# Spectral mixing kernel: step 1 of the forward transform as 49 by 64, its float16 products on quarters of the TensorE array

## The chip, the cores and the metric

The kernel runs on one core of one Trainium2 chip. The metric is the device time of one execution in microseconds; the median of three runs is compared. A profiled execution has a span (first to last instruction) and a time of its own; both are given below.

## The reference

```python
# x: (8, 3136, 256); w_r, w_i: (256, 256); moe: d_model 256, d_ff 1024
X = np.fft.rfft(x, axis=1)
Yr = Xr @ w_r - Xi @ w_i + b_r
Yi = Xr @ w_i + Xi @ w_r + b_i
Yr, Yi = soft_threshold(Yr, 0.01), soft_threshold(Yi, 0.01)
y = np.fft.irfft(Yr + 1j * Yi, n=3136, axis=1)
h = y.reshape(25088, 256) @ w_in
sm = softmax(h)                       # along the 1024 columns
solu = h * sm
ln = (solu - mean) / np.sqrt(var + 1e-06) * g_ln
out = ln @ w_out
...
```

## The kernel before

The eight sequences (batches b = 0 to 7) go through the same stages. The transform of length 3136 is split as 98 by 32. **Step 1** (`fwd1`, for batches 2 to 7; `fwd1_plain` with float32 products for batches 0 and 1) multiplies a 98 by 98 matrix of cosines and sines, `fa16_s`, with x laid out as 98 rows; eight chunks of 1024 columns make a batch. In `fwd1` a chunk is loaded into `xt`, split into two float16 parts `xh` (by ScalarE) and `xl` (by VectorE), multiplied in two halves of 512 columns with three products each, and each half is taken out of PSUM as two float16 parts into `av` (ScalarE writes the high part, VectorE the low part). `av` goes to DRAM as `s1`. **Step 2** (`fwd2`) reads `s1` back as `bin`, in groups of four (`load_bin`), and multiplies with `fb`; its result `Xh`, `Xl` is mixed with the weights (`mix`), thresholded, transformed back (`inv1` with `gb`, whose 64 by 128 products run on the two row halves of the array at a time, and `inv2` with `ia_s`), and written to a ring `ring_hi`, `ring_lo` of 128-row tiles.

The second part takes 196 such tiles: `moe_head` (products `ph` with `win`, six per half, row maximum `nm`, exponential, sums), `moe_turn` (float16 parts `lh` and `ll`, two transposing DMAs to `th` and `tl`) and `moe_tail` (24 products `po` with `wout`, scaling, store). A batch is 24 or 25 tiles; while the tiles of batch b run, step 1 of batch b+2 and step 2 to `inv1` of batch b+1 run among them.

The order is made before the program is built: each operation is recorded with a key (`nc.key`, a place in tiles), and a planner (`Plan`) puts the operations of all engines in one order by keys, data, buffers and PSUM banks, with lengths of its own for each operation. Each engine then executes its list strictly in that order. All DMAs are issued by one queue, SyncE's (SP), in its order; they use eight semaphores in turn, so a DMA is not issued before the one eight places ahead of it has landed. PSUM has eight banks; at most five hold front results (`pf`), five `ph`, two `po`.

Before the change a `pf` bank is asked for one half of a chunk at a time, and `xt` has four buffers, used in turn by the chunk loads of step 1 and by `load_peak` (which reads a batch once, to find its largest value). All recorded operations are issued from one line, L342 (L349 after the change), so in the profile they are told apart by the names of their tiles; there `fa16_s` stands as `fa_s`, and `s1`, `s2` of the float16 batches as `s`.

Of the kernel before, what the change touches and what calls it, by code (L numbers as in the profile page):

```python
# [25 lines left out]
H = N1 // 2  # L26
Q = (H - 1) // 2
# [5 lines left out]
S_SCALE, B_SCALE, Z_SCALE, X_SCALE = 2.0**-7, 2.0**-5, 2.0**-11, 2.0**-11  # L33
# [6 lines left out]
def fft_constants():  # L40
# [5 lines left out]
    FA, IA = np.zeros((N1, N1)), np.zeros((N1, N1))  # L46
    comps = []
    for q in range(Q):
        comps += [(2 * q + 1, 0), (2 * q + 2, 0), (2 * q + 1, 1), (2 * q + 2, 1)]
    comps += [(0, 0), (H, 0)]  # L50
    for c, (k1, im) in enumerate(comps):
        t = 2 * np.pi * ((np.arange(N1) * k1) % N1) / N1
        FA[:, c] = -np.sin(t) if im else np.cos(t)
        IA[c, :] = (1.0 if k1 in (0, H) else 2.0) / S * (-np.sin(t) if im else np.cos(t))

    def angle(k):
        return 2 * np.pi * ((np.arange(N2)[:, None] * np.asarray(k)[None, :]) % S) / S
# [3 lines left out]
    for q in range(Q):  # L61
        for j in range(2):
            k = 2 * q + 1 + j + N1 * np.arange(N2)
            s = np.where(2 * k > S, -1.0, 1.0)[None, :]
            C, Sn = np.cos(angle(k)), np.sin(angle(k))
            re, im = slice(j * N2, (j + 1) * N2), slice((2 + j) * N2, (3 + j) * N2)
            FB[re, q, re], FB[im, q, re] = C, Sn
            FB[re, q, im], FB[im, q, im] = -Sn * s, C * s
            GB[re, q, re], GB[im, q, re] = C.T, -(Sn * s).T
            GB[re, q, im], GB[im, q, im] = Sn.T, (C * s).T  # L70
    kd, kn = N1 * np.arange(1, N2 // 2), H + N1 * np.arange(N2 // 2)
    nd, m = len(kd), len(kd) + len(kn)
    FS, GS = np.zeros((2 * N2, P)), np.zeros((P, 2 * N2))
    d, n, I = slice(0, N2), slice(N2, 2 * N2), 2 * N2
    alt = np.cos(np.pi * np.arange(N2))
    FS[d, 0:nd], FS[n, nd:m], FS[d, m], FS[d, m + 1] = np.cos(angle(kd)), np.cos(angle(kn)), 1.0, alt
    FS[d, I : I + nd], FS[n, I + nd : I + m] = -np.sin(angle(kd)), -np.sin(angle(kn))
# [12 lines left out]
    out = dict(fa=FA.astype(np.float32), fbf=FB.astype(np.float32), fsf=FS.astype(np.float32))  # L90
    out["iaf"] = (IA * IA_SCALE).astype(np.float32)
    parts = dict(fa16=FA * A_SCALE, fb=FB, fs=FS, gb=GB * G_SCALE, gs=GS * G_SCALE, ia=IA * IA_SCALE)
# [132 lines left out]
class Op:  # L225
    def __init__(self, engine, key, seq):
        self.engine, self.key, self.seq = engine, key, seq
        self.calls, self.length, self.moved, self.tiles = [], 0.0, 0.0, []
        self.needs, self.next, self.start, self.end, self.half, self.port = set(), [], None, None, False, False
# [7 lines left out]
class Plan:  # L237
# [60 lines left out]
    def weigh(self, op, name, args, kw, ins, outs):  # L298
# [6 lines left out]
        elif op.engine == "tensor":  # L305
            moving = ins[-1]
            n = moving.cells.size * (4 if moving.dtype == F32 else 1) * 0.42 + 1
            op.half = "gb" in ins[0].tile.kw["name"]
            op.length += n / 2 if op.half else n
# [34 lines left out]
    def order(self):  # L344
        ready = {e: [] for e in self.ENGINES}
        free = dict.fromkeys(self.ENGINES, 0.0)
        waits, bus, half, port = {}, 0.0, False, 0.0
# [35 lines left out]
        while len(done) < len(self.ops):  # L383
# [15 lines left out]
            if e == "tensor":  # L399
                if op.half != half:  # L400
                    at += 100.0 if op.half else 220.0
                half = op.half
# [49 lines left out]
def fft_mix_solu_kernel(ctx: ExitStack, tc, x, w_r, w_i, b_r, b_i, w_in, w_out, g_ln, fa, fbf, fsf, iaf, fa16, fb, fs, gb, gs, ia, out):  # L452
# [70 lines left out]

    def load_after(t, src, before):

        nc.hold(before)
        nc.sync.dma_start(t, src)
# [8 lines left out]
    def load_peak(b, c):  # L536

        n = S * D // P // NPK
        t = xp.tile([P, C1], F32, name="xt", bufs=4)[:, :n]
# [41 lines left out]
    def fwd1(b, c):  # L581
        if c == 0:
            s1[b] = dram.tile([N1, N2, 2, D], F16, name="s1")
        xt = xp.tile([P, C1], F32, name="xt", bufs=4)[:N1]
        nc.sync.dma_start(xt, x[b].rearrange("(n1 n2) d -> n1 (n2 d)", n1=N1)[:, c * C1 : (c + 1) * C1])
        xh = xp.tile([N1, C1], F16, name="xh")
        xl = xp.tile([N1, C1], F16, name="xl")
        k = scales[b]["x"][:N1]
        nc.scalar.activation(xh, xt, AF.Copy, scale=k)
        nc.vector.scalar_tensor_tensor(xl, xt, k, xh, ALU.mult, ALU.subtract)  # L590
        n2 = C1 // D
        av = xp.tile([P, n2, 2, D], F16, name="av")[:N1]
        for h in range(C1 // HF):
            hs = slice(h * HF, (h + 1) * HF)
            pa = front_psum(b)
            nc.reserve(av[:, h * HF // D : (h + 1) * HF // D])
            with nc.together():
                for i, (t, j) in enumerate(((xh, 0), (xh, 1), (xl, 0))):
                    nc.tensor.matmul(pa[:N1], fa16_s[:, j], t[:, hs], start=i == 0, stop=i == 2)
            pv = pa[:N1].rearrange("p (n d) -> p n d", d=D)  # L600
            ah, al = (av[:, h * HF // D : (h + 1) * HF // D, j] for j in range(2))
            nc.scalar.activation(ah, pv, AF.Copy, scale=S_SCALE / A_SCALE)
            nc.vector.scalar_tensor_tensor(al, pv, S_SCALE / A_SCALE, ah, ALU.mult, ALU.subtract)
        nc.sync.dma_start(s1[b][:, c * n2 : (c + 1) * n2], av)
# [3 lines left out]
    def fwd1_plain(b, c):  # L608


        if c == 0:
            s1[b] = dram.tile([N1, N2, D], F32, name="s1f")
        n2 = C1 // D
        pool, name, bufs = (mp, "u", 4) if b == 0 and c % 2 == 0 else (xp, "xt", 4)
        xt = pool.tile([P, C1], F32, name=name, bufs=bufs)[:N1]
# [19 lines left out]
        for av, i, n in parts:  # L635
            nc.sync.dma_start(s1[b][:, c * n2 + i : c * n2 + i + n], av.rearrange("p (n d) -> p n d", d=D))
# [587 lines left out]
```

## Time and profile before

| | before |
|---|---|
| median of 3 runs | 1614.72 us (1614.09 to 1615.25) |
| profiled execution: time | 1616.65 us |
| profiled execution: span | 1614.9 us |
| busy PE / DVE / ACT / POOL | 98% / 82% / 77% / 70% |
| mean granted TensorE clock | 0.990 |

The profiled execution's time is 1.75 us above its span and 1.93 us above the median of the runs. Busy time of PE counts each matmul from its start to its modelled end, and ends overlap the following starts; how long a stream of matmuls takes is therefore read from the distance between starts.

### The profile page before, as it was taken

Reading aid. Unit: us, or ns where it says so; the run is one execution under the profiler, and the core shown is the slowest. Engines: PE = TensorE matmul, PEld = TensorE weight load, DVE = VectorE, ACT = ScalarE, POOL = GpSimd, SP = SyncE. Lnnn points to the kernel's source line nnn. Section 1 sums busy time; section 2 is a strip of 40 time slices with the busy share of each in tenths; the row PEclk is TensorE's granted clock in tenths of the full one; section 3 lists DMA queues with packets and bytes.
Section 4 is the critical chain, followed back from the end, with each engine's and each line's share of the span. In section 5 each row is a group of like instructions: output and inputs, shape, how many; then the busy total and the mean of one; then the engine's idle time right before and its main releaser. Section 6 shows DMA issues by size and latency. Waiting matters only on the chain.

```text
span 1614.9 us, 38042 instructions
## 1 busy us (share of the span) xinstructions
PE 1577.4 (98%) x13040; PEld 1126.1 (70%) x13040; DVE 1326.1 (82%) x3423; ACT 1238.8 (77%) x2576; POOL 1123.6 (70%) x1889
## 2 busy tenths in 40 slices
PE   5979999999999999999999999999999999999998
PEld 3545877678766777667776687666876677776675
DVE  4779789996799877898789978899688888877775
ACT  4667678886789867898679876798678877778886
POOL 0555776677866777667777687766976677777676
PEclk8989999999999999999999999999999999999999
DMA  8868955996579965899669984699857986677676
GB/s 236 277 228 206 210 145 133 227 240 155 127 185 232 226 151 121 185 243 217 135 130 224 279 169 118 135 246 258 166 112 165 204 172 129 122 146 154 140 129 115
DMA packets 533923, 290.25 MB, mean 180 GB/s; under 512 B 427642, under 2 KB 503964, under 8 KB 533728
## 3 DMA queue, kind: packets, MB, share of 16 engines
q1 hardware_dynamic: 533728, 287.82, 78.5%
q8 instruction: 102, 1.67, 0.4%
q14 instruction: 93, 0.76, 0.2%
HBM read 107.89 MB, written 77.07 MB: 115 GB/s over the span
## 4 chain that ended last, share of the span: by engine, by line
PE 92%; DVE 3%; ACT 2%; DMA 1%; issue 1%; POOL 0%; SPq 0%; DVEq 0%; ACTq 0%; POOLq 0%
PE po L342 31%; PE ph L342 30%; PE pf L342 27%; PE pb L342 4%; DVE u L342 1%; DVE xl L342 1%; DVE nm L342 1%; DMA zt<-s2f 0%; ACT u L342 0%; DMA s2f<-zs 0%; ACT junk L342 0%; DMA bin<-s1f 0%; DMA s1f<-tl 0%; DVE av L342 0%; DMA th<-lh 0%
## 5 line engine op out<-in xcount | busy, mean ns | idle before, releaser
L342 POOL TENSOR_TENSOR ll<-u,lh 128x1024 f16<-128x1024 f32 x196 | 424.4, 2166 | 98.5 <-ACT lh L342 95.4
L342 PE MATMUL po<-wout,th 128*128 128x256 f16 x3136 | 374.5, 273 | 4.1 <-DMA th<-lh 1.9
L342 PEld LDWEIGHTS <-th 128*128 128x128 f16 x3136 | 305.4, 98 | 64.9 <-issue 4.4
L342 ACT ACTIVATE u<-ph,m,hsb 128x512 f32<-128x512 f32 x384 | 295.9, 776 | 52.3 <-DVE m L342 51.7
L342 DVE TENSOR_REDUCE nm<-ph 128x1 f32<-128x512 f32 x392 | 264.5, 685 | 79.7 <-PE ph L342 78.6
L342 DVE SCALAR_TENSOR_TENSOR u<-ph,ch,u 128x512 f32<-128x512 f32 x392 | 281.5, 747 | 23.1 <-ACT u L342 13.7
L342 PE MATMUL ph<-win_hi,ring_hi 128*128 128x512 f16 x768 | 291.9, 380 | 0.2 <-DVE u L342 0.2
L342 PE MATMUL ph<-win_lo,ring_hi 128*128 128x512 f16 x768 | 291.5, 380 | 0.0
L342 PE MATMUL ph<-win_low,ring_lo 128*128 128x512 f16 x768 | 291.3, 379 | 0.0
L342 ACT CAST lh<-u 128x1024 f16<-128x1024 f32 x196 | 205.7, 1049 | 53.1 <-DVE u L342 52.8
L342 PEld LDWEIGHTS <-ring_hi 128*128 128x128 f16 x1536 | 146.8, 98 | 140.5 <-issue 6.5
L342 ACT ACTIVATE junk<-u,total 128x1024 bf16<-128x1024 f32 x196 | 226.1, 1154 | 7.1 <-POOL total L342 6.6
L342 PE MATMUL po<-wout,tl 128*128 128x256 f16 x1568 | 203.4, 273 | 0.8 <-DMA tl<-ll 0.8
L342 PEld LDWEIGHTS <-tl 128*128 128x128 f16 x1568 | 150.7, 98 | 35.0 <-issue 3.4
L342 POOL TENSOR_TENSOR y<-yt,yc 128x512 f32<-128x512 f32 (+1 forms) x104 | 133.1, 1281 | 59.4 <-ACT yt L342 32.7
L342 POOL TENSOR_TENSOR yl<-y,yh 128x512 f16<-128x512 f32 (+1 forms) x104 | 122.3, 1178 | 40.3 <-ACT yh L342 39.3
L342 PE MATMUL pf<-w_hi,Xh 128*128 128x256 f16 (+1 forms) x546 | 149.1, 273 | 0.0
L342 PE MATMUL pf<-w_hi,Xl 128*128 128x256 f16 (+1 forms) x546 | 148.9, 273 | 0.0
L342 PE MATMUL pf<-w_lo,Xh 128*128 128x256 f16 (+1 forms) x546 | 148.8, 273 | 0.0
L342 ACT ACTIVATE o<-po,r 128x256 f32<-128x256 f32 x196 | 93.2, 475 | 59.6 <-PE po L342 30.7
L342 PEld LDWEIGHTS <-ring_lo 128*128 128x128 f16 x768 | 75.1, 98 | 91.1 <-DVE last_lo L342 0.3
L342 PEld LDWEIGHTS <-Xh 128*128 128x128 f16 (+1 forms) x1196 | 113.9, 99 | 24.8 <-issue 1.9
(196 smaller groups left out, 2922.5 us busy)
## 6 DMA issues: line engine op xcount, KB each, us to landing
xt<-in_x_dram SPq DMA_DIRECT2D x108, 392.0 KB
zt<-s SPq DMA_DIRECT2D x56, 392.0 KB
s<-zout SPq DMA_DIRECT2D x42, 512.0 KB
s<-av SPq DMA_DIRECT2D x48, 392.0 KB
bin<-s SPq DMA_DIRECT2D x36, 512.0 KB
out_dram<-o SPq DMA_DIRECT2D x128, 96.0 KB
out_dram<-o SPq DMA_DIRECT2D x136, 64.0 KB
bin<-s1f SPq DMA_DIRECT2D x12, 512.0 KB
```

What stands on the lines that cost most here:

```text
L342: getattr(engine, name)(*args, **kw)
```

## The change

Step 1 becomes 49 by 64. Its matrix has 49 rows and columns, x is read as 49 rows of 64 by 256 values, and step 2 has 64 inputs for each of 49 components where it had 32 for each of 98 (its matrices keep their size of 128 by 128). The 49 by 49 matrix of the float16 batches is held twice, in partitions 0 to 48 and 64 to 112. A chunk holds the same 98 by 1024 values as before, as two blocks of 49 rows in partitions 0 to 48 and 64 to 112; each product of a chunk is four matmuls of 49 by 49 by 512, one for each quarter (row half r, column half g) of the array. Row halves write to different PSUM banks, column halves to different partitions of one bank. Two chunks are put together: their 24 matmuls are one group in PE's order, which asks for four banks at a time. Loads and stores of 49 rows are issued as 48 rows and one, so a chunk has four loads and four stores where it had one each. `xt` is now four fixed places: step 1 uses two, `load_peak` the two others. The rows 49 to 63 of step 1's places are cleared once by GpSimd. The batches with float32 products keep 98 by 98 matmuls, with a matrix that does two parts in one.

The keys change too: step 1 has 13 steps per batch (8 peaks, the scales, 4 pairs) from `first + 2` instead of 17 from `first + 6`, `front_b` starts one tile earlier, and `moe_tail` has its key half a tile later. The planner counts a quarter matmul as a fourth of its columns.

```diff
+    both = np.zeros((2 * F1, 2 * F1))
+    both[::2, ::2] = both[1::2, 1::2] = FA
+    quarters = np.zeros((P // 2 + F1, P // 2))
+    quarters[:F1, :F1] = quarters[P // 2 :, :F1] = FA
...
+            op.split = 2 if "gb" in name else 4 if name == "fa16_s" else 1
+            op.length += n / op.split
...
-        t = xp.tile([P, C1], F32, name="xt", bufs=4)[:, :n]
+        t = x_place(2, 3)[:, :n]
...
+    def fwd1(b, c0):
+
+        if c0 == 0:
+            s1[b] = dram.tile([F1, F2, 2, D], F16, name="s1")
+        half = P // 2
+        R = half + F1
+        xv = x[b].rearrange("(n1 c g r i) d -> c r n1 g (i d)", n1=F1, g=2, r=2, i=2)
+        k = scales[b]["x"][:R]
+        work = []
+        for c in range(c0, c0 + TOGETHER):
+            xt = x_place(0, 1)[:R]
+            for r in range(2):
+                for rows in rows_apart(r):
+                    n1 = slice(rows.start - r * half, rows.stop - r * half)
+                    nc.sync.dma_start(xt[rows].rearrange("p (g m) -> p g m", g=2), xv[c, r][n1])
+            xh = xp.tile([P, C1], F16, name="xh")[:R]
+            xl = xp.tile([P, C1], F16, name="xl")[:R]
+            nc.scalar.activation(xh, xt, AF.Copy, scale=k)
+            nc.vector.scalar_tensor_tensor(xl, xt, k, xh, ALU.mult, ALU.subtract)
+            av = xp.tile([P, 2, 2, 2, D], F16, name="av")[:R]
+            work.append((c, xh, xl, av, [front_psum(b) for _ in range(2)]))
+        nc.reserve(*(w[3] for w in work))
+        with nc.together():
+            for _, xh, xl, _, pa in work:
+                for i, (t, j) in enumerate(((xh, 0), (xh, 1), (xl, 0))):
+                    for r in range(2):
+                        rows = slice(r * half, r * half + F1)
+                        for g in range(2):
+                            nc.tensor.matmul(
+                                pa[r][g * half : (g + 1) * half], fa16_s[rows, j], t[rows, g * HF : (g + 1) * HF], start=i == 0, stop=i == 2
+                            )
+        for c, _, _, av, pa in work:
+            for r in range(2):
+                pv = pa[r][:R].rearrange("p (n d) -> p n d", d=D)
+                ah, al = av[:, r, :, 0], av[:, r, :, 1]
+                nc.scalar.activation(ah, pv, AF.Copy, scale=S_SCALE / A_SCALE)
+                nc.vector.scalar_tensor_tensor(al, pv, S_SCALE / A_SCALE, ah, ALU.mult, ALU.subtract)
+            for g in range(2):
+                to = s1[b][:, 8 * c + 4 * g : 8 * c + 4 * g + 4].rearrange("k n t d -> k (n t d)")
+                for rows in rows_apart(g):
+                    nc.sync.dma_start(to[rows.start - g * half : rows.stop - g * half], av[rows].rearrange("p r i t d -> p (r i t d)"))
+
+    TOGETHER = 2
...
-        steps = [(load_peak, (b, c)) for c in range(NPK)] + [(set_scales, (b,))] + [(fwd1, (b, c)) for c in range(NCH)]
+        steps = [(load_peak, (b, c)) for c in range(NPK)] + [(set_scales, (b,))] + [(fwd1, (b, c)) for c in range(0, NCH, TOGETHER)]
...
+            clear_between()
         if b + 2 < B:
-            front_a(b + 2, first + 6, (L - 6) / 17)
+            front_a(b + 2, first + 2, (L - 2) / 13)
         if b + 1 < B:
-            front_b(b + 1, first + (6 if b == 0 else -2), (L - (8 if b == 0 else 4)) / (NU + 3))
+            front_b(b + 1, first + (6 if b == 0 else -3), (L - (8 if b == 0 else 5)) / (NU + 3))
...
-            nc.key = first + n + 1
+            nc.key = first + n + 1.5
```

On PE, the first chunk of step 1 in batch 2 stood before the change like this (names with their numbers, so that the PSUM banks `pf` can be told apart):

```order
L342 LDWEIGHTS fa16_s_171
L342 MATMUL pf_3436<-xh_3277,fa16_s_171 98x512
L342 LDWEIGHTS fa16_s_171
L342 MATMUL pf_3436<-xl_3392,fa16_s_171 98x512
L342 LDWEIGHTS fa16_s_171
L342 MATMUL pf_3440<-xh_3277,fa16_s_171 98x512
L342 LDWEIGHTS fa16_s_171
L342 MATMUL pf_3440<-xl_3392,fa16_s_171 98x512
```

The first of its two `xh` products on each bank is not shown twice; a chunk was six matmuls with six weight loads. With the change the first pair of chunks begins like this on PE:

```order
L349 MATMUL ph_3890<-win_low_1105,ring_lo_1233 128x512
L349 LDWEIGHTS fa16_s_168
L349 MATMUL pf_3901<-xh_3476,fa16_s_168 64x512
L349 LDWEIGHTS fa16_s_168
L349 MATMUL pf_3904<-xh_3476,fa16_s_168 64x512
L349 LDWEIGHTS fa16_s_168
L349 MATMUL pf_3901<-xl_3552,fa16_s_168 64x512
L349 LDWEIGHTS fa16_s_168
L349 MATMUL pf_3904<-xl_3552,fa16_s_168 64x512
L349 LDWEIGHTS fa16_s_168
L349 MATMUL pf_3915<-xh_3524,fa16_s_168 64x512
```

Each matmul row stands there twice in a row (the two column halves), and the `xh` rows once more for the second product: 24 matmuls on four banks follow each other, with a weight load ahead of each, and no other product stands among them.

On SP, the end of step 1 of batch 4 stood before the change like this, from the last stores of `av` to the first load of `bin`:

```order
L342 DMA s1_10713<-av_11439 98x2048
L342 DMA zt_11522<-s2_8997 98x2048
L342 DMA_TRANSPOSE th_11579<-lh_11550 128x8x128
L342 DMA xt_11600<-in_x_dram 128x784
L342 DMA_TRANSPOSE tl_11618<-ll_11577 128x8x128
L342 DMA out_0_dram<-o_11616 96x256
L342 DMA out_0_dram<-o_11616 32x256
L342 DMA xt_11658<-in_x_dram 128x784
L342 DMA_TRANSPOSE th_11670<-lh_11646 128x8x128
L342 DMA xt_11690<-in_x_dram 98x1024
L342 DMA xt_11705<-in_x_dram 98x1024
L342 DMA bin_11709<-s1_10713 128x4x512
```

And with the change, for the same batch:

```order
L349 DMA s1_11053<-av_11996 48x2048
L349 DMA s1_11053<-av_11996 1x2048
L349 DMA out_0_dram<-o_12024 32x256
L349 DMA out_0_dram<-o_12024 96x256
L349 DMA_TRANSPOSE th_12090<-lh_12011 128x8x128
L349 DMA out_0_dram<-o_12101 96x256
L349 DMA out_0_dram<-o_12101 32x256
L349 DMA_TRANSPOSE tl_12152<-ll_12027 128x8x128
L349 DMA bin_12174<-s1_11053 128x4x512
```

The store rows of 48 and of one stand there twice for each of two chunks, eight in a row. Behind the last of them the first load of `bin` has moved from the eleventh issue behind it to the seventh, and no load of `xt` stands between. In the whole program SP issues 1480 DMAs where it issued 1192.

## Rows read from the trace of the kernel before

**Rows 1.** Page, busy us (share of the span) and instructions of each engine.
```profile
PE 1577.4 (98%) x13040; PEld 1126.1 (70%) x13040; DVE 1326.1 (82%) x3423; ACT 1238.8 (77%) x2576; POOL 1123.6 (70%) x1889
```
**Rows 2.** Page, shares of the span in the chain that ended last.
```profile
PE 92%; DVE 3%; ACT 2%; DMA 1%; issue 1%; POOL 0%; SPq 0%; DVEq 0%; ACTq 0%; POOLq 0%
```
**Rows 3.** Busy us of the engines in stretches of the span.
```profile
core 0: us, PE busy (x) PEld busy (x) DVE busy (x) ACT busy (x) POOL busy (x), PEclk, DMA share, GB/s
...
200.00:1500.00 1300.00, 1296.62 (x11129) 938.95 (x11128) 1103.79 (x2858) 1023.49 (x2138) 942.35 (x1595) 1.00 0.79 176
...
660.00:735.00 75.00, 74.33 (x536) 48.28 (x535) 72.33 (x195) 67.98 (x139) 47.70 (x98) 1.00 1.04 237
```
**Rows 4.** Tile `fa_s`: operation, count, ns min/median/max, first and last start us.
```profile
L342 PE MATMUL pf<-xh,fa_s x192: 377/379/418, 256.8 to 1279.5; 98*98 98x512 f16 x192
L342 PE MATMUL pf<-xl,fa_s x96: 376/378/379, 257.3 to 1279.7; 98*98 98x512 f16 x96
```
**Rows 5.** Timeline of PE around one chunk of step 1: start us, us, work.
```profile
303.82 0.60 PE L342 MATMUL pf<-xh,fa_s 98*98 98x512 f16 x2
...
304.47 0.59 PE L342 MATMUL pf<-xh,fa_s 98*98 98x512 f16 x2
...
305.12 0.38 PE L342 MATMUL ph<-win_hi,ring_hi 128*128 128x512 f16 x1
```
**Rows 6.** Timeline of PE around 24 products with `gb`, on row halves.
```profile
370.63 0.49 PE L342 MATMUL po<-wout,th 128*128 128x256 f16 x3
371.06 0.39 PE L342 MATMUL pf<-yh,gb 64*128 64x256 f16 x4
371.29 0.38 PE L342 MATMUL pf<-yl,gb 64*128 64x256 f16 x4
...
372.47 0.39 PE L342 MATMUL po<-wout,tl 128*128 128x256 f16 x2
```
**Rows 7.** Timeline of weight loads (PEld) in the stretch of rows 6.
```profile
371.05 1.21 PEld L342 LDWEIGHTS <-gb 64*128 64x128 f16 x24 [0.21 <-issue]
```
**Rows 8.** Timeline of PE around six products with `gs_s`, all on one quarter.
```profile
301.74 0.40 PE L342 MATMUL pf<-yh,gs_s 64*64 64x256 f16 x2
301.99 0.38 PE L342 MATMUL pf<-yl,gs_s 64*64 64x256 f16 x2
...
302.51 0.39 PE L342 MATMUL ph<-win_hi,ring_hi 128*128 128x512 f16 x1
```
**Rows 9.** Groups of instructions, ACT, of 98 and of 128 partitions: busy us, mean ns.
```profile
L342 ACT ACTIVATE av<-pf 98x512 f16<-98x512 f32 x96 | 56.1, 603 | 9.5 <-PE pf L342 7.6 <-ACT junk L342 1.0
L342 ACT ACTIVATE Xh<-pf 128x512 f16<-128x512 f32 x72 | 43.2, 600 | 0.0
```
**Rows 10.** Timeline of PE, the longest wait of step 1: in brackets idle us, releaser.
```profile
481.82 0.59 PE L342 MATMUL pf<-xh,fa_s 98*98 98x512 f16 x2 [1.46 <-DVE u L342]
```
**Rows 11.** Tile `s`, SP's issues: ns min/median/max.
```profile
L342 SPq DMA_DIRECT2D s<-av x48: 307/367/1154, 260.5 to 1283.0; - x48
```
**Rows 12.** Timeline of SP from the last store of step 1 to step 2's load.
```profile
714.42 0.69 SPq L342 DMA_DIRECT2D s<-av  x1
715.21 0.34 SPq L342 DMA_DIRECT2D zt<-s  x1
...
725.34 0.40 SPq L342 DMA_DIRECT2D bin<-s  x1
```
**Rows 13.** Timeline of PE, last step-1 and first step-2 matmul, batch 4, then 7.
```profile
706.55 0.38 PE L342 MATMUL pf<-xl,fa_s 98*98 98x512 f16 x1
...
735.91 0.83 PE L342 MATMUL pf<-fb,bin 128*128 128x128 f16 x12
...
1279.71 0.38 PE L342 MATMUL pf<-xl,fa_s 98*98 98x512 f16 x1
...
1296.39 0.78 PE L342 MATMUL pf<-fb,bin 128*128 128x128 f16 x11
```

More of the change, by code (lines that the diff above doesn't have):

```diff
@@ L88, in fft_constants @@
     GS = GS.reshape(2, 2 * N2, 2 * N2).transpose(1, 0, 2)
-    out = dict(fa=FA.astype(np.float32), fbf=FB.astype(np.float32), fsf=FS.astype(np.float32))
+    both = np.zeros((2 * F1, 2 * F1))
+    both[::2, ::2] = both[1::2, 1::2] = FA
+    quarters = np.zeros((P // 2 + F1, P // 2))
+    quarters[:F1, :F1] = quarters[P // 2 :, :F1] = FA
+    out = dict(fa=both.astype(np.float32), fbf=FB.astype(np.float32), fsf=FS.astype(np.float32))
     out["iaf"] = (IA * IA_SCALE).astype(np.float32)
-    parts = dict(fa16=FA * A_SCALE, fb=FB, fs=FS, gb=GB * G_SCALE, gs=GS * G_SCALE, ia=IA * IA_SCALE)
+    parts = dict(fa16=quarters * A_SCALE, fb=FB, fs=FS, gb=GB * G_SCALE, gs=GS * G_SCALE, ia=IA * IA_SCALE)
     out.update({k: halves(v) for k, v in parts.items()})
@@ L228, in __init__ @@
         self.calls, self.length, self.moved, self.tiles = [], 0.0, 0.0, []
-        self.needs, self.next, self.start, self.end, self.half, self.port = set(), [], None, None, False, False
+        self.needs, self.next, self.start, self.end, self.split, self.port = set(), [], None, None, 1, False
     def touch(self, tile):
@@ L307, in weigh @@
             n = moving.cells.size * (4 if moving.dtype == F32 else 1) * 0.42 + 1
-            op.half = "gb" in ins[0].tile.kw["name"]
-            op.length += n / 2 if op.half else n
+            name = ins[0].tile.kw["name"]
+            op.split = 2 if "gb" in name else 4 if name == "fa16_s" else 1
+            op.length += n / op.split
         else:
@@ L346, in order @@
         free = dict.fromkeys(self.ENGINES, 0.0)
-        waits, bus, half, port = {}, 0.0, False, 0.0
+        waits, bus, split, port = {}, 0.0, 1, 0.0
         for op in self.ops:
@@ L522, in fft_mix_solu_kernel, with x_place, clear_between @@
     s1 = {}
+    places = const.tile([P, 4, C1], F32, name="xt")
+    turns = {}
+    def x_place(*some):
+        turns[some] = turns.get(some, -1) + 1
+        return places[:, some[turns[some] % len(some)]]
+    def clear_between():
+        nc.gpsimd.memset(places[P // 4 : P // 2, :2], 0.0)
     def load_after(t, src, before):
@@ L579, in set_h_scale @@
         scales[b]["h"] = hs
[L581 to L597, printed above, removed]
-                for i, (t, j) in enumerate(((xh, 0), (xh, 1), (xl, 0))):
[L599 to L604, printed above, removed]
```

66 lines of the change are left out of this document (34 added, 32 removed).

## The prediction

> **What bounds the kernel now.** I read the page's busy shares first: PE is busy 98% of the span, VectorE, the next, 82% [rows 1]. Then the chain that ended last: 92% of the span lies on PE [rows 2]. So the span is the length of PE's stream, and the question for each part is whether PE streams less or waits more. The third view says where PE waits today: from 200 to 1500 us it is busy 1296.62 of 1300 us at a granted clock of 1.00, so it loses 3.4 us in that stretch [rows 3]. All of step 1 in float16 lies in it, from 256.8 to 1279.7 us [rows 4]. The same view shows who is close behind: in one stretch of step 1, 660 to 735 us, VectorE is busy 72.3 of 75 us, ScalarE 68.0, and the DMA engines are full (share 1.04) [rows 3]. A microsecond taken from PE there is a microsecond of the kernel only if these keep up, and that decides how much of the gain stays.
>
> **What is removed.** Step 1 has 192 + 96 = 288 matmuls of 512 columns [rows 4], six per chunk in 48 chunks. The first of a chunk starts at 303.82 us and the first matmul behind the chunk at 305.12: 1.30 us per chunk [rows 5]. 48 x 1.30 = 62.4 us leave the stream.
>
> **What is added on PE.** A product of a chunk is now four matmuls of 512 columns on four quarters, with the column count of one old half. If the four run together, a product takes as long as one old matmul, 1.30 / 6 = 0.217 us, and 48 x 3 = 144 products take 31.2 us. No row shows two column halves at work together. The nearest shows row halves: four `gb` matmuls of 256 columns take 0.23 us, 371.06 to 371.29, where the full-array `po` of 256 columns in front of them take 0.109 each, so two run at a time [rows 6]. The bounds are therefore 31.2 us (four at a time) and 62.4 us (row halves together, column halves one after the other). I take four at a time: `gb` shows that the array accepts parts as independent streams, and column halves of one row half read other columns of the same rows and write to other partitions of the same bank. *The Trainium skill, "TensorEngine Tiling (Array Packing)", section "Available Configurations", counts 64 by 64 as four tiles; no row of this case shows four at work.*
>
> Weight loads double to 576, each for 49 columns. The 24 loads of `gb` start and end within 1.21 us, 0.05 us each [rows 7], so four loads per product need 0.20 of its 0.217 us if they need as long; 49 columns are fewer than the 128 there. I cost them at nothing; the cover is the product before them. Without it they cost up to 0.20 us per product, 29 us in all.
>
> Changing between whole array and parts costs time. The last `po` in front of `gb` starts at 370.63 + 2 x 0.109 = 370.85, `gb` at 371.06, the next `po` at 372.47 [rows 6]: 1.62 us for one `po` (0.109) and twelve pairs (1.31), so 0.20 us to go in and out. 24 groups: 4.8 us.
>
> PE's stream changes by 31.2 + 4.8 - 62.4 = **-26.4 us**. That is the gain if nothing new waits.
>
> **What the other engines get.** ScalarE and VectorE have as many instructions as before on 113 partitions instead of 98; 98 partitions take 603 ns and 128 take 600 [rows 9], so nothing. The clearing is one GpSimd instruction in the whole program, on an engine that is busy 942 of 1300 us [rows 3]; nothing. DMA bytes stay the same, with half as long pieces on the load side; at a full DMA system that could cost or gain, and I put it to the waits below. SP issues 288 DMAs more, at the 0.367 us of a store of step 1 [rows 11], taken for loads and stores alike: 106 us of queue time, 18 per batch. In the stretch behind step 1 SP is already full: from the store at 714.42 to the load at 725.34 eleven issues follow with about 0.1 us between them [rows 12]. Queued behind the new issues are the transposes whose result `po` needs, and `bin`, which step 2 needs.
>
> **New waits.** (a) A group wants four PSUM banks and both chunks' `xl` at once, where a half wanted one bank. The longest wait for step 1 today is 1.46 us [rows 10]. (b) Step 2 follows step 1 sooner. In batch 4 the last step-1 matmul starts at 706.55 us and the first of step 2 at 735.91, 29.4 us later; in batch 7 it is 16.7 us, 1279.71 to 1296.39, and PE does not wait [rows 13]. In the order of the change there stand, between the two in batch 4, 42 products `ph` (0.217 us), 56 `po` (0.109) and 24 with `ia_s` (0.046, an estimate by its 98 columns): 16.3 us; counted so, the six batches have 16 to 20 us. That is about the shortest chain that the trace shows to go well, and now four banks are taken out and eight stores issued in it. What is late next is all of PE, since its list is strict. For (a) and (b) together the lower bound is 0 (the planner moved work so that it fits) and the upper has no row; 24 groups that each wait the 1.46 us would be 35 us. I take six such waits, one per batch: **+8.8 us**, nearer to the low end, because today's order loses only 3.4 us in 1300 us though SP and VectorE are as full in these stretches.
>
> **Sum.** -26.4 + 8.8 = -17.6 us. On the profiled execution: 1614.9 - 17.6 = 1597.3 us span, 1599.0 us with the 1.75 us around it. Against the runs' median of 1614.72 us, 1.9 us below that execution, the forecast is **1597 us**.
>
> **Rivals.**
>
> *Waits take most of it.* The queue on SP is the likeliest place: if the 18 us of issues per batch find no gaps, transposes and `bin` come late by a part of that. With 3 to 4 us per batch instead of 1.5, 18 to 24 us are lost and the time is 1606 to 1612 us. For it: SP is full behind step 1 [rows 12], DMA share 1.04 [rows 3]. Against it: these full stretches cost PE nothing now, and no peak load of x stands any more between stores and `bin`.
>
> *Slower: the parts do not all overlap.* If the column halves of a row half take turns, 144 products take 62.4 us, PE's stream grows by 4.8 us, and with 4 to 9 us of waits the time is 1623 to 1628 us. It decides when a group of 24 takes over 2.4 us instead of 1.3 + 0.2: at 2.6 + 0.2 nothing is saved. The same end is reached if weight loads cannot hide: the two column halves use the same rows, so a load would wait for the matmul in flight on the other half, and with 0.20 us per product the 26.4 us are gone and 2.4 more (1617 us; 1626 with the waits). Against it: the six `gs_s` products, all on one quarter and so in the same rows, each with its own load, start 0.12 us apart, about the 0.109 of a 256-column matmul, so loads hide behind a matmul in the same rows [rows 8]. *The Trainium skill, "TensorE: Matmul & The Clock Gate", section "The mechanism" in Part 3, says that a weight load overlaps with matmuls in flight only when its row group differs; by that rule this rival would hold and the time would be the 1626 us above. The six products [rows 8] do not bear the rule out.*
>
> *Slower by SP alone.* Over 4.4 us of lateness per batch (26.4 / 6) the gain is gone; if all 18 us of issues came through, the time would be 1614.7 - 26.4 + 108 us. SP would have to have no gap at all; I give the part above 1618 us little.
>
> *All of it stays.* No new waits: 1588 us.
>
> **How the numbers follow.** Four at a time with 0 to 17 us of waits (1588 to 1605 us): 0.66, forecast 1597 within it. Waits of 17 to 23 us (1605 to 1611): 0.14. Waits that cancel the gain (1611 to 1618): 0.07. Slower by the parts: 0.07, by SP: 0.05. Better than 1588, by waits of today that go: 0.01. The range of 8 in 10 is the first two cases, 1587 to 1611 us. About 0.2% (3.2 us) is what a measurement of this kernel can tell from no change: faster 0.81, same 0.07, slower 0.12.
>
> **What would show it.** Right: in the timeline groups of 24 `fa_s` matmuls with about 1.5 us from the first start to the next work, four starts within some nanoseconds; in 200 to 1500 us some 10 us of idle PE, at step 1's and step 2's first matmul. Wrong: fours that start 0.2 us apart inside a product (parts in turn, or loads in the open); long waits of PE on `th`, `tl` or `bin` (SP); a granted clock below 1.00 in those stretches, which I have left out.

## The result, and the profile after

The changed kernel takes 1625.33 us (median of 4 runs, 1623.24 to 1627.11) against 1614.55 us of the kernel before in runs beside it: ratio 1.0066, 95% interval 1.0048 to 1.0083. The forecast was 1597 us, range 1587 to 1611. The profiled span went from 1614.9 to 1625.1 us.

The page's busy shares and the chain that ended last, changed kernel [rows 1, 2 before]:

```profile
PE 1564.6 (96%) x13328; PEld 1107.1 (68%) x13328; DVE 1332.9 (82%) x3423; ACT 1242.8 (76%) x2576; POOL 1121.0 (69%) x1890
PE 79%; DMA 7%; DVE 5%; ACT 4%; issue 2%; POOL 1%; SPq 1%; DVEq 0%; ACTq 0%; POOLq 0%
```

PE works 13 us less in a span 10 us longer. In the chain PE's share fell from 92 to 79%, and DMA's rose from 1 to 7%. The stretch of [rows 3]:

```profile
core 0: us, PE busy (x) PEld busy (x) DVE busy (x) ACT busy (x) POOL busy (x), PEclk, DMA share, GB/s
200.00:1500.00 1300.00, 1272.97 (x11369) 913.37 (x11367) 1101.47 (x2837) 1021.55 (x2127) 936.03 (x1584) 0.99 0.80 175
```

PE stands idle for 27 of 1300 us where it was 3.4, and the granted clock is no longer 1.00. The view of PE's waits (from 200 us; us in total, times, longest) says for what:

```profile
PE po L349 <- DMA th<-lh: 17.1, 13, 4.6
PE po L349 <- DMA tl<-ll: 9.1, 10, 1.5
```

Before, the same two lines:

```profile
PE po L342 <- DMA th<-lh: 1.9, 2, 1.6
PE po L342 <- DMA tl<-ll: 0.8, 1, 0.8
```

Step 1 itself runs as forecast. PE's timeline of one group (start us, us, work) and the tile `fa_s` (count: ns min/median/max) [rows 4, 5]:

```profile
286.21 0.38 PE L349 MATMUL ph<-win_low,ring_lo 128*128 128x512 f16 x1
286.52 0.63 PE L349 MATMUL pf<-xh,fa_s 49*64 49x512 f16 x8
286.98 0.39 PE L349 MATMUL pf<-xl,fa_s 49*64 49x512 f16 x4
287.19 0.60 PE L349 MATMUL pf<-xh,fa_s 49*64 49x512 f16 x8
287.62 0.39 PE L349 MATMUL pf<-xl,fa_s 49*64 49x512 f16 x4
287.94 1.05 PE L349 MATMUL po<-wout,tl 128*128 128x256 f16 x8
...
L349 PEld LDWEIGHTS <-fa_s x576: 102/107/173, 286.5 to 1302.2; 49*64 49x64 f16 x192
L349 PE MATMUL pf<-xh,fa_s x384: 372/376/632, 286.5 to 1302.2; 49*64 49x512 f16 x192
```

24 matmuls take 1.42 us from the first start to the next work (286.52 to 287.94); two chunks took 2.60. The weight loads of `gb` in the kernel before, for comparison:

```profile
L342 PEld LDWEIGHTS <-gb x1152: 92/94/96, 52.5 to 1416.6; 64*128 64x128 f16 x192
```

Where the 10.2 us come from, by my own sums over the starts of neighbouring matmuls from 200 us to the end (the time of a matmul is its columns at 2.4 GHz; what lies beyond it goes to the matmul that follows, or, in a stretch of granted clock 0.5, to that stretch, together with the waits in it):

| us | before | after | difference |
|---|---|---|---|
| step 1's matmuls | 62.3 | 32.2 | -30.1 |
| mode changes | 8.9 | 13.6 | +4.7 |
| waits at step 1's matmuls | 2.4 | 0.8 | -1.6 |
| waits at `po` | 5.0 | 24.7 | +19.7 |
| lost in stretches at 1.2 GHz, their waits included | 0 | 14.7 | +14.7 |
| all else | | | +2.8 |

Of the 14.7 us, 6.9 are two further waits at `po` (4.59 and 2.32 us by the timeline) that reach into such stretches. The slower clock itself costs the rest, about 7.8 us, so waits at `po` come to 31.6 us in all.

One of the waits from its beginning, changed kernel: ScalarE's, SP's and PE's timelines (start us, us, work, in brackets the idle time and its releaser) and the stretch behind it:

```profile
897.94 1.12 ACT L349 CAST lh<-u 128x1024 f16<-128x1024 f32 x1
...
898.86 1.28 SPq L349 DMA_TRANSPOSE tl<-ll  x1
900.24 3.05 SPq L349 DMA_DIRECT2D s<-av  x8
903.41 0.79 SPq L349 DMA_DIRECT2D out_dram<-o  x2
904.25 4.81 SPq L349 DMA_DIRECT2D xt<-in_x_dram  x8
909.16 1.17 SPq L349 DMA_DIRECT2D out_dram<-o  x2
910.43 1.29 SPq L349 DMA_TRANSPOSE th<-lh  x1
...
911.06 0.38 PE L349 MATMUL pf<-v,ones 1*128 1x2 f32 x2
913.76 3.53 PE L349 MATMUL po<-wout,th 128*128 128x256 f16 x16 [2.32 <-DMA th<-lh]
917.13 1.04 PE L349 MATMUL po<-wout,tl 128*128 128x256 f16 x8
...
913.68:917.10 3.42, 3.34 (x16) 2.40 (x17) 3.42 (x18) 2.57 (x6) 1.49 (x6) 0.50 1.03 193
```

`lh` is ready at 899.06. Its transpose is issued at 910.43, behind eight stores (3.05 us) and eight loads (4.81 us) of step 1 and four stores of the result. PE waits 2.32 us, and then sixteen `po` take 3.37 us (913.76 to 917.13) instead of 16 x 0.109 = 1.74, because the granted clock of that stretch is 0.50, which is 1.2 GHz. Between 200 and 1500 us there are three such stretches. The first begins in a wait at `po` (4.59 us, ending at 321.47), the second at the end of the one shown, the third 1.3 us behind one of 2.59 us; before there was none.

Over all 372 transposes from 200 us on, the time from ready data to the issue sums to 719 us (before: 339). SP stands still in 117 of it and issues other DMAs in the rest; step 1's loads and stores and the peak loads take 204 (before: 43). SP as a whole is not full: from 200 us on it issues for 977 of 1425 us. In the rest it waits, by the view of its waits mostly for other engines' results that the next DMA in its order needs. The rule of eight semaphores is not what holds it: only 22 of its issues, with 13 us of standing in all, follow within 0.3 us on the landing of the DMA eight places ahead (e2: 5 issues, 4 us).

### The profile page after: what moved, and what is told of

It reads as the page before. It is cut to its first block, busy times and chain, and to the rows that moved or that the text cites. A ratio compares the mean times of both kernels' runs of the same rounds, so it can differ in the third digit from the quotient of the medians.

```text
span 1625.1 us, 39102 instructions
## 1 busy us (share of the span) xinstructions
PE 1564.6 (96%) x13328; PEld 1107.1 (68%) x13328; DVE 1332.9 (82%) x3423; ACT 1242.8 (76%) x2576; POOL 1121.0 (69%) x1890
## 4 chain that ended last, share of the span: by engine, by line
PE 79%; DMA 7%; DVE 5%; ACT 4%; issue 2%; POOL 1%; SPq 1%; DVEq 0%; ACTq 0%; POOLq 0%
PE po L349 27%; PE ph L349 24%; PE pf L349 23%; PE pb L349 4%; DMA th<-lh 3%; DMA tl<-ll 2%; DVE u L349 1%; ACT u L349 1%; SPq L349 1%; DVE nm L349 1%; POOL ll L349 1%; ACT junk L349 1%; DVE xl L349 1%; ACT lh L349 0%; DMA zt<-s2f 0%
## 5 line engine op out<-in xcount | busy, mean ns | idle before, releaser
L349 PE MATMUL po<-wout,th 128*128 128x256 f16 x3136 | 379.7, 275 | 18.2 <-DMA th<-lh 18.0
L349 POOL TENSOR_TENSOR y<-yt,yc 128x512 f32<-128x512 f32 (+1 forms) x104 | 136.6, 1314 | 69.8 <-ACT yt L349 33.1
```

The costliest lines, as they stand in the source:

```text
L349: getattr(engine, name)(*args, **kw)
```

## The experiments

Theory A: SP is short of time where it counts; step 1's additional issues make `th` and `tl` late, PE waits at `po`, and behind the longer waits its clock falls. Rivals: the new order (keys) leaves `po` too little lead; the small DMAs burden the DMA engines; the quarters themselves cost.

All runs in one table. "Order" says whether PE, VectorE, ScalarE and GpSimd have the order of the kernel that was edited or the planner made a new one. The columns behind it: DMAs of step 1; SP's issuing time from 200 us (sum of its DMA records); mean time from ready `lh` to the issue of `th`; the time from the landing of `th` (its last semaphore event) to when PE is free for it, the value that 5% of the tiles stay under; waits at `po` and loss at 1.2 GHz (waits in those stretches included) as above. They come from one profiled execution each; those of e12 and e17 took 7 us more than the run's median, that of e1 5.5 more and that of e15 5 less. The last column has the median, and the ratio to runs of the kernel before beside it (medians 1613.65 to 1616.73 us). e7 and e17 have no landing figure, since two queues share the eight semaphores there.

| run | order | DMAs | SP us | delay | slack 5% | `po` | 1.2 GHz | us, ratio to before [95%] |
|---|---|---|---|---|---|---|---|---|
| before | | 96 | 896 | 0.84 | 0.95 | 5.0 | 0 | 1614.55 |
| after | | 384 | 977 | 1.82 | -0.55 | 24.7 | 14.7 | 1625.33, 1.0066 [1.0048, 1.0083] |
| e1 49 rows in one | kept | 192 | 994 | 1.83 | -1.48 | 47.6 | 27.8 | 1657.25, 1.0265 [1.0239, 1.029] |
| e2 before + 288 | kept | 96+288 | 1035 | 3.20 | -1.58 | 52.1 | 8.6 | 1681.91, 1.0415 [1.0392, 1.0438] |
| e3 old keys | new | 384 | 974 | 1.81 | -1.44 | 34.1 | 17.4 | 1640.36, 1.0156 [1.0129, 1.0182] |
| e4 `po` later | new | 384 | 972 | 1.65 | -0.86 | 28.1 | 18.6 | 1634.31, 1.0117 [1.0098, 1.0136] |
| e5 one-row left out | kept | 192 | 924 | 0.99 | 0.22 | 6.9 | 4.3 | 1605.35, 0.9937 [0.9919, 0.9954] |
| e6 two chunks per DMA | new | 192 | 992 | 1.61 | -0.68 | 44.1 | 16.3 | 1657.29, 1.0269 [1.0244, 1.0294] |
| e7 one-row from ScalarE | new | 384 | 922 | 0.82 | | 23.7 | 26.7 | 1648.08, 1.0207 [1.0183, 1.023] |
| e8 one chunk at a time | new | 384 | 994 | 1.72 | -0.82 | 33.3 | 7.2 | 1639.4, 1.0154 [1.0124, 1.0184] |
| e9 52 rows in one | kept | 208 | 934 | 1.13 | 0.22 | 8.4 | 14.8 | 1612.6, 0.9984 [0.9975, 0.9994] |
| e10 no loads | kept | 96 | 861 | 0.86 | 0.82 | 5.7 | 7.4 | 1601.78, 0.9915 [0.9897, 0.9933] |
| e11 stores behind | kept but SP | 384 | 985 | 1.72 | -0.64 | 33.9 | 28.8 | 1668.73, 1.0316 [1.0294, 1.0339] |
| e12 52 rows, stores behind | kept but SP | 208 | 929 | 1.27 | -0.16 | 20.9 | 18.0 | 1634.11, 1.0129 [1.0106, 1.0152] |
| e13 one out store | kept | 384 | 879 | 1.16 | 0.24 | 10.7 | 1.6 | 1604.3, 0.9923 [0.9908, 0.9938] |
| e14 before, one out store | kept | 96 | 800 | 0.59 | 1.02 | 5.1 | 0 | 1615.75, 0.9996 [0.9986, 1.0006] |
| e15 52 rows, new order | new | 208 | 959 | 1.40 | -0.59 | 29.4 | 3.3 | 1636.53, 1.012 [1.0097, 1.0143] |
| e16 52 rows, GpSimd | kept | 208 | 849 | 0.84 | 0.29 | 9.2 | 7.5 | 1606.95, 0.9939 [0.9918, 0.9961] |
| e17 52 rows, ScalarE | kept | 208 | 849 | 0.81 | | 8.1 | 16.5 | 1608.34, 0.9961 [0.9945, 0.9978] |

**e1.** The planner sees 48 and one; what is issued is one DMA of 49 rows (loads alike).

```diff
...
+                ops[0].calls = [("dma_start", (to, av[rows].rearrange("p r i t d -> p (r i t d)")), {})]
+                ops[1].calls = []
```

> The changed kernel with its order of instructions on all engines kept; only the 49 rows of a half move as one DMA instead of 48 and one, so step 1 issues 192 DMAs where the changed kernel issues 384 (before: 96). Theory A (SP: the additional issues stand in front of the transposes th and tl, po comes late, PE waits and its clock drops behind the longer waits): with two thirds of the additional issues gone the waits of PE at po fall from 24.7 us to 8-15, the time at 1.2 GHz from 14.7 to under 6, and the time is 1598-1612 us. Theory B (the order: the new keys leave po fewer tiles of lead, whatever SP has to issue): nothing changes, 1621-1628 us. Theory C (moving 48 rows is what lands quickly; 49 rows in one DMA land late): step 1 itself waits, 1625 us or more.

Slower by 32 us than the changed kernel. A as I had put it (counting issues) failed; the time is theory C's, but not the place: step 1 waits no longer than in the changed kernel, and it is `po` that waits twice as long. PE's waits, e1:

```profile
PE po L349 <- DMA th<-lh: 39.4, 23, 6.5
PE po L349 <- DMA tl<-ll: 15.1, 12, 3.8
```

Tile `s`, SP's issues (ns min/median/max), changed kernel, then e1:

```profile
L349 SPq DMA_DIRECT2D s<-av x192: 221/309/1294, 291.3 to 1309.5; - x192
```
```profile
L349 SPq DMA_DIRECT2D s<-av x96: 268/481/2919, 288.6 to 1344.3; - x96
```

Half as many stores take SP as long (96 x 0.71 us mean = 69 us against 192 x 0.35 = 67). A 49-row store lands 5.6 us after its issue (median), a 48-row one 3.0. A 49-row DMA raises its semaphore in 8 events, a 48-row one in 16. The Trainium skill, "DMA: Bandwidth & Descriptors", section "Why a DMA increments its semaphore by 16 and not by 1", says that a DMA is split over the largest number of engines up to 16 that divides the slowest dimension of both its sides, and that the rest of the count comes at once: by that, seven engines for 49 rows, and seven events and one. The trace agrees, for 98 rows (15 events), 52 (14) and one row of a store (2) too. Fewer engines would fit the late landing, but no run separates that. The longer issue is only in part due to the 49 rows: a 48-row store without its one-row companion (e5) holds SP for 0.58 us, a 52-row one (e9) for 0.60.

**e2.** In the kernel before, behind each load and store of step 1:

```diff
...
+                for _ in range(3 if op in self.idlers else 0):
+                    self.nc.sync.dma_start(*next(self.more))
...
```

> The kernel before with its order of instructions kept, and three more DMAs of 4 KB (DRAM to DRAM, read by nobody) behind each load and each store of step 1: 288, the number that the change adds. Theory A (SP issues): transposes come late as in the changed kernel, the waits at po rise from 5.0 us to 15-30 and the clock may drop behind the longer ones: 1622-1650 us. Theory B (the order alone): 1612-1618 us, as the kernel before.

Theory A; 67 us, more than expected, at an issue of 0.63 us mean. PE's waits, e2:

```profile
PE po L347 <- DMA th<-lh: 34.4, 28, 3.7
PE po L347 <- DMA tl<-ll: 12.7, 15, 1.8
```

No quarter and no new order is needed for these waits, only a fuller SP.

**e3, e4.** Two edits of the keys:

```diff
-            nc.key = first + n + 1.5
+            nc.key = first + n + 1
...
-            front_b(b + 1, first + (6 if b == 0 else -3), (L - (8 if b == 0 else 5)) / (NU + 3))
+            front_b(b + 1, first + (6 if b == 0 else -2), (L - (8 if b == 0 else 4)) / (NU + 3))
```
```diff
-            nc.key = first + n + 1.5
+            nc.key = first + n + 2.5
```

> The changed kernel with the keys of the kernel before for po (one step behind its tile instead of one and a half) and for the second step of the forward transform; the keys of step 1 stay new. Theory B (the new keys cause the waits): the waits at po fall towards the 5 us of before and the time is 1595-1608 us. Theory A (SP issues): the transposes stay late, and po with an earlier key waits as long or longer: 1620-1640 us.

> The changed kernel with the key of po one more step later (2.5 instead of 1.5 steps behind its tile), so that the planner may put the ph of another tile in front of it. Theory A (SP's bursts make th and tl 2 to 5 us late): a further tile of PE work (about 4 us with its share of the other steps) in front of po covers most of it; waits at po fall from 24.7 us to 5-12 and the time is 1596-1610 us. If the planner's own time for po, and not the key, decides where it stands: 1620-1628 us. If the longer life of th and of its two other buffers makes the transposes wait in turn: slower than 1628 us.

Both slower. The old keys do not help, as A had expected; since the whole order is new there, this run alone does not clear the new keys (e10 does). A later `po` did not cover the lateness, which A had expected it to. e4's time lies in the third case, but its transposes are not issued later (1.65 against 1.82 us after `lh` is ready), so the reason given there is not seen.

**e5.** The planner sees 48 and one as in e1, but the one-row DMAs are not issued (loads alike; the rows in DRAM that nothing writes any more are filled once).

```diff
...
+                    op.calls = op.calls if rows.stop - rows.start > 1 else []
```

> The changed kernel with its order of instructions kept on all engines, and the 192 DMAs of a single row left out (the 49th row of each half is neither loaded nor stored, so that frequency's result is not the reference's); 48-row DMAs stay. Step 1 issues 192 DMAs instead of 384, and none of them is a 49-row one. Theory A (SP's issues in front of the transposes): SP has 60 to 70 us less to issue, waits at po fall from 24.7 us to 8-14 and the time at 1.2 GHz from 14.7 us to under 6: 1598-1610 us. Theory B (the order alone, with PE simply ahead of its transposes): waits stay, 1620-1627 us.

Theory A: SP issues 53 us less (60 to 70 expected), the waits at `po` fall to 6.9, below the 8 to 14 expected, and 20 us come back in an unchanged order.

**e6, e7, e8.** Three ways to ease SP, each with a new order: the loads and stores of both chunks in one DMA; the one-row DMAs from ScalarE; `TOGETHER = 1`, with 17 steps per batch instead of 13.

```diff
...
-                for rows in rows_apart(r):
+        for r in range(2):
+            for rows in rows_apart(r):
+                nc.sync.dma_start(xts[rows].rearrange("p c (g m) -> p (c g) m", g=2), xw[r, n1])
...
```
```diff
-                    nc.sync.dma_start(...
+                    (nc.sync if rows.stop - rows.start > 1 else nc.scalar).dma_start(...
```
```diff
-    TOGETHER = 2
+    TOGETHER = 1
...
-            front_a(b + 2, first + 2, (L - 2) / 13)
+            front_a(b + 2, first + 2, (L - 2) / 17)
```

> The changed kernel with both chunks of a group in one DMA (four loads and four stores per group of two chunks, still as 48 rows and one): 192 DMAs for step 1 instead of 384, the planner makes its order anew. Theory A (SP): as much relief as leaving the one-row DMAs out, 1598-1612 us, if twice as long DMAs land in time. Theory B (the order alone): a new order may fall either way, 1615-1635 us, with no relation between the waits and the number of issues.

> The changed kernel with the 192 DMAs of a single row issued by ScalarE's queue instead of SP's, order made anew by the planner. Theory A (SP): the transposes stand behind half as many issues; waits at po 8-15 us, 1600-1613 us, unless ScalarE, which now stands still for the issues and their waits, makes u, lh and so th later itself (then 1620 us or more, with PE's waits still at th but the transposes no longer late behind their data). Theory B (the order alone): 1615-1635 us.

> The changed kernel with groups of one chunk (12 matmuls on quarters, two PSUM banks) spread over the batch, as many DMAs as the changed kernel, but in bursts of four instead of eight. Mode changes double (48 groups: 4.8 us more on PE). Theory A with the length of a burst as what counts: waits at po fall to 10-15 us, 1608-1618 us. Theory A with the number of issues as what counts: waits stay at 20-28 us, 1625-1635 us.

None helped. e6 did not ease SP (992 us: a store of two chunks costs 0.80 us, two of one chunk 0.70) and came out above both ranges. e7 did (922), and its transposes are issued as early as before, but PE waits as long: the exception that its expectation names. The trace shows part of the reason: ahead of 25 of its issues ScalarE stands for 32 us in all, and goes on within 0.3 us of the landing of a DMA of SP that has the same semaphore. How much of PE's waiting follows from that, no run separates. e8 leaves SP as full, in shorter bursts, and is slower than both its cases.

**e9, e10.** 52 rows in one DMA, which raise their semaphore in 14 events; the order is kept (the last batch's loads stay 48 and one, so there are 208 DMAs). e10 also leaves out step 1's loads.

```diff
...
+    TOGETHER, ROWS = 2, 52
...
+                    rows = slice(r * half, r * half + ROWS)
+                    ops[0].calls = [("dma_start", (xt[rows].rearrange("p (g m) -> p g m", g=2), xv52[c, r]), {})]
+                    ops[1].calls = []
...
```

> The changed kernel with its order of instructions kept; 52 rows move in one DMA instead of 48 and one (the three rows too many hold values that nothing reads), so step 1 issues 208 DMAs instead of 384, and none spreads over as few DMA engines as 49 rows did. Theory A (what counts is how long SP issues step 1's DMAs in front of the transposes, and 49 rows failed because they landed late and blocked the queues): about as good as leaving the one-row DMAs out, waits at po 6-12 us, 1602-1612 us, faster than both kernels. Rival (any row count that is moved as one loses, because the one-row DMA let the transposes pass, or because the bytes count): 1620 us or more.

> As the 52-row kernel, and step 1's loads of x left out altogether (it computes with what lies in its places; the result is not the reference's): 96 DMAs for step 1, as many as in the kernel before, and 20 MB less to move. Theory A: the lateness of the transposes and the waits at po come back to those of before (about 5 us), no clock loss: 1590-1600 us, the gain of the quarters as predicted without new waits 1588. Rival (PE's waits come with the quarters or with the order themselves): waits at po stay above 10 us, 1605 us or more.

e9's waits at `po` outside slow stretches are as expected. It is about level with the kernel before (0.16% faster), 0.6 us above the range that A gave; the profiled run still lost 14.8 us in stretches at 1.2 GHz, in or behind two waits of 2.5 and 2.9 us and at the start, behind a wait of 1.8 us for VectorE's `v`. PE's waits, e10:

```profile
PE po L349 <- DMA th<-lh: 2.3, 2, 1.6
PE po L349 <- DMA tl<-ll: 0.6, 1, 0.6
```

e10 has before's waits at `po` (5.7 against 5.0) and gains 14 us, in the order of the changed kernel: the order and the quarters alone do not make `po` wait. It is 1.8 us above A's range, since a loss at 1.2 GHz is left that A had put at nothing. The quarters' gain is real where SP has time.

**e11, e12.** Each store of step 1 moves behind the transposes that follow it within eight issues on SP; nothing else moves.

```diff
...
+            for o in queue[n + 1 : n + 1 + self.REACH]:
+                if o in op.next:
+                    break
+                if any(kw.get("transpose") for _, _, kw in o.calls):
+                    to = o
...
```

> The changed kernel with all 384 DMAs of step 1 and the same order on PE, VectorE, ScalarE and GpSimd; only on SP each store of step 1 stands behind the transposes that followed it within eight issues. Theory A (the place in SP's queue: step 1's issues in front of transposes that PE needs sooner): the stores' part of the lateness goes, waits at po fall from 24.7 us to 10-18 us, 1606-1618 us. Rival (the number of DMAs as such, their load on the DMA engines and their descriptors, wherever they stand): the waits stay, 1621-1628 us. Rival (SP now stands at a transpose whose data is not ready, and loads behind it come late): PE waits at step 1 instead, 1620 us or more.

> The 52-row kernel with its stores of step 1 behind the transposes as in the run before. Theory A: both reliefs add up in part; waits at po 3-7 us, 1603-1611 us against 1612.6 of the 52-row kernel alone. Rival (number of DMAs as such): 1610-1615 us, as the 52-row kernel.

My expectation failed in both. PE's waits, e11:

```profile
PE pf L350 <- DMA bin<-s: 15.7, 6, 3.4
PE po L350 <- DMA th<-lh: 15.6, 14, 3.0
PE po L350 <- DMA tl<-ll: 9.5, 13, 1.8
```

The waits at `th` and `tl` stay (26.2 before the move, 25.1 now), and 15.7 us at step 2's `bin`, which needs the stores, come on top. The move hardly brought the transposes forward (1.72 us after `lh` is ready instead of 1.82); it made something else late as well.

**e13, e14.** SP is relieved of DMAs that are not step 1's: one store per tile of the result, in the changed kernel and in the one before.

```diff
...
+            op.calls = [("dma_start", (out[b * S + t * P : b * S + (t + 1) * P], o), {})] if p + n == P else []
```

> The changed kernel with its order kept and step 1 untouched (384 DMAs, 48 rows and one); each tile of 128 rows of the result leaves in one DMA instead of two or three, to consecutive rows of the output (the rows land in the wrong places, so the output is not the reference's; as many bytes). SP has about 190 issues less, none of them of step 1: about 100 us. If it is SP's time that is short, whichever DMAs take it: waits at po fall from 24.7 us to 6-14, 1600-1613 us. If it is the small DMAs of step 1 as such (their descriptors, their bursts in the DMA engines): waits stay at 18-25 us, 1618-1627 us.

> The control to the run before: the same edit in the kernel before, in its order. It waits 5 us at po, so it has at most that and some of the 11 us of other waits to win: 1608-1615 us. If it wins as much as the changed kernel does by the same edit, SP's time is not what sets the two kernels apart.

The pair decides between SP's time and step 1's DMAs as such. Stretch 200 to 1500 us and PE's waits, e13, then the stretch of e14:

```profile
200.00:1500.00 1300.00, 1290.43 (x11546) 929.15 (x11544) 1118.32 (x2889) 1038.11 (x2166) 955.90 (x1617) 1.00 0.81 177
...
PE po L349 <- DMA th<-lh: 3.7, 5, 1.9
PE po L349 <- DMA tl<-ll: 2.6, 4, 1.3
```
```profile
200.00:1500.00 1300.00, 1296.62 (x11132) 939.32 (x11131) 1103.77 (x2859) 1023.38 (x2138) 941.15 (x1594) 1.00 0.79 176
```

With all 384 DMAs of step 1 and SP at 879 us, 21 us come back and PE is idle 9.6 of 1300 us. The DMA engines are as busy as in the changed kernel (share 0.81 and 0.80). The same relief (96 us) gives the kernel before nothing, and its row reads as in [rows 3]: it had SP time to spare.

**e15, e16, e17.** e9 with an order made anew; e9 with the second piece of each tile's result issued by GpSimd, or by ScalarE.

```diff
...
+            if p:
+                op.queue = "gpsimd"
...
```

> The 52-row kernel with the order made anew by the planner, which now counts 192 DMAs of step 1 instead of 384. If the planner's order answers to SP's load: 1600-1612 us. If a new order falls either way, as the orders of the runs with other keys did (1634 to 1657 us): 1615-1650 us, although SP has as little to issue as in the 52-row kernel with the order kept (1612.6 us).

> The 52-row kernel (1612.6 us) with its order kept, and the second piece of each tile's result (about 190 DMAs) issued from GpSimd's queue instead of SP's; everything is computed and stored as the reference wants. If SP's time is what is short: both reliefs together, waits at po 3-6 us, 1592-1603 us, faster than both kernels. If GpSimd, which makes ll and so tl, loses more by issuing than SP gains: PE waits at tl instead, 1612 us or more.

> The same with the second pieces issued from ScalarE's queue, which makes their data o itself. If only SP's time counts: 1592-1603 us. If ScalarE's standing at an issue (it makes lh and u) or the DMA lanes that both queues share cost more: PE waits at th or ph again, 1612 us or more, as in the run that gave ScalarE the one-row DMAs (1648 us, with a new order).

e15: with as many DMAs as e9 (SP issues for 959 us instead of 934), the new order costs 24 us. e16 computes and stores everything and is faster than both kernels (0.9939 of before). GpSimd pays for it and has the time; stretch 200 to 1500 us, e16:

```profile
200.00:1500.00 1300.00, 1286.37 (x11502) 925.22 (x11501) 1119.04 (x2881) 1035.38 (x2155) 1046.63 (x1778) 1.00 0.82 178
```

GpSimd is busy 1046.6 us there instead of 936.0. e17 does nearly as well in its median, so ScalarE's queue need not cost what it cost in e7. It is not harmless: three of its ten runs took 1614 us or more, the profiled one (1615.5) among them. There ScalarE stands 5.0 us at an issue, until a `zt` load of SP with the same semaphore has landed, and PE waits for ScalarE's `Xh` (ScalarE's timeline, then PE's):

```profile
558.25 0.60 ACT L349 ACTIVATE Xh<-pf 128x512 f16<-128x512 f32 x1 [5.37 <-DMA zt<-s]
...
558.91 0.40 PE L349 MATMUL pf<-w_hi,Xh 128*128 128x256 f16 x1 [3.85 <-ACT Xh L349]
```

Both stop short of the 1592 to 1603 us expected, since waits of 2 us and more and stretches at 1.2 GHz remain. The Trainium skill, "DMA: Bandwidth & Descriptors", section "Issuing engines are not separate DMA queues", says that issuing from several engines saves only the sequencer's time, usually small beside the DMA. That it saves just this fits e16; here that time is not small: 977 us of SP in 1425.

## Why the prediction was wrong, point by point

- **Removed and added on PE**: right. Forecast -62.4 + 31.2 = -31.2; measured -30.1. By the starts of single matmuls in the trace, fours start within some 10 ns, and the next four 0.21 us later.
- **Mode changes**: right, 4.7 us against 4.8.
- **Weight loads at nothing**: right in result, wrong in the reading. A load takes 0.107 us. The 0.05 was the spacing of the `gb` loads, two of which ran at a time; each of them took 0.094 in the trace of before. Four one after the other (0.43) would not fit under a product of 0.217, so they overlap each other as well. *The Trainium skill, "TensorE: Matmul & The Clock Gate", section "The mechanism" in Part 3, lets a load overlap only matmuls of another row group; each of the four shares its rows with another here, and the trace does not agree. That section of the Trainium skill also lets a load to the background weight buffer go ahead; no trace here shows which buffer a load goes to.* The rival that rested on it gave 1626 us, one us from the result, but its condition (a group of 24 over 2.4 us) is not met at 1.42. That it came so close is luck: a right total is no evidence for a cause.
- **ScalarE and VectorE, memset, DMA bytes at nothing**: right (1242.8 and 1332.9 us busy against 1238.8 and 1326.1).
- **SP, 106 us**: right in size. Loads to `xt` (the peak loads among them) and stores from `av` took SP 67 us from 200 us on and take 184, 117 more. The one price for all was not right: a one-row load holds SP for 0.62 us (mean), a one-row store for 0.32.
- **New waits, +8.8 us**: this step failed. I put them at step 1's and step 2's first matmuls, (a) and (b). There PE waits 1.6 us less than before, and at `bin` not at all. I had named the transposes behind step 1's issues and then given them no term. The wait stands at `po`, for those transposes: 19.7 us more outside the slow stretches and 14.7 in them, of which 6.9 are waits at `po` too and about 7.8 the clock, which I had left out. Together that is 34.4 us where I had 8.8, or 34.4 / 6 = 5.7 us per batch. That is the rival "slower by SP alone", which I had let begin at 4.4 us and given 0.05.
- **Why I thought it unlikely**: "SP would have to have no gap at all", and "these full stretches cost PE nothing now". The first is wrong: SP issues for 977 of 1425 us, and the waits came in bursts. And no wait is not the same as room. The trace of before could have said how much room there was: `th` lands 2.7 us (median) and 0.95 us (5% of the tiles) before PE is free for it, while a burst of eight issues takes 3 to 5 us (3.05 and 4.81 in the lines above). e14 and e2 show the two sides of that edge: 96 us taken from SP give the kernel before nothing, 139 us more cost it 67.

What stays open: why orders made anew do worse with as many DMAs on SP (e15 against e9; their slack at 5% is -0.59 and 0.22 us), and why some waits of PE are followed by a stretch at 1.2 GHz and others are not. What e10 still loses so (7.4 us) stands behind a wait of 1.8 us for VectorE's `v`, at 314 us, and one of 1.6 us at `po` at the very end.

## What to carry to other kernels

When a change adds DMAs to a queue that something critical shares, compare the length of its bursts with the slack of the transfers queued behind them (landing to first use), tile by tile; an idle time of nought on the consumer says nothing about it. Give work to a queue by its issue time, not by the number of DMAs, and measure that time in the kernel as it will be: one DMA of 49 rows (0.71 us) or of two chunks (0.80) cost SP as much as the two that it stood for (0.70). When a re-planned variant disappoints, keep the order fixed and change one thing.

## What the runs showed of the hardware that was not expected

- A store of 49 rows lands in 5.6 us (median) and holds SP for 0.71 us (mean). One of 52 rows takes 3.6 and 0.60 (e9), one of 48 rows 3.4 and 0.58 (e5); with a one-row store behind each, 48 rows take 3.0 and 0.38. So the time that an issue takes hangs on what stands around it.
- A load of one row (4 KB) holds SP for 0.62 us (mean), one of 48 rows (192 KB) for 0.45.
- Behind 200 us, the stretches of PE at 1.2 GHz in these traces, as far as matmuls lie in them, begin in a wait of PE or within 1.4 us behind one. Not every long wait has one: in e1 waits of 2.6 and 2.8 us have none, in the changed kernel one of 2.3 us has. What the clock takes is half of the stretch's work time (3.37 us for 1.74).
- Where two engines issue DMAs on the same eight semaphores, one can stand for the other's DMA: ScalarE 5.0 us in e17, 32 us in e7.
- Four quarters with a weight load of 0.107 us each run as fast as one full-array matmul of as many columns (0.216 us each in the group at 286.52).
